# Attention and a top-1 mixture of experts on one core: routing steps kept in line, three batches counted, scatters between products, gate sums on ScalarE and VectorE

## The chip, the core and the metric

The kernel runs on one core of a Trainium2 chip. The metric is the device time of one execution in microseconds (us), as the median of several runs. A core has TensorE (PE, matrix products), VectorE (DVE), ScalarE (ACT), GpSimd (POOL), SyncE (SP, which here issues most of the DMAs) and DMA queues. Each engine follows its own list of instructions, and semaphores make one wait for another.

## What is computed

Cut to what matters:

```python
# attention: q, k, v are (8, 8, 576, 64): batches, heads, positions, width
scores = (1 / sqrt(64)) * q @ k.transpose(0, 1, 3, 2)
scores = where(block_i >= block_j, scores, -1e9)      # blocks of 64 positions
scores = scores - scores.max(-1, keepdims=True)
attn = exp(scores); attn = attn / (attn.sum(-1, keepdims=True) + 1e-9)
x = (attn @ v) .transpose(0, 2, 1, 3).reshape(4608, 512)
# top-1 mixture of 8 experts
logits = x @ w_gate + modality_bias[modality_id]      # w_gate is 512 x 8
e_idx = argmax(logits, axis=1)
probs = exp(logits - max); probs /= probs.sum(-1) + 1e-9
gate_w = probs[arange(N), e_idx]
for e in range(8):                                    # w1 is 512 x 1024, w2 1024 x 512
    mask = e_idx == e
    h = maximum(x[mask] @ w1[e], 0)
    out[mask] = gate_w[mask, None] * (h @ w2[e])
```

The tokens are routed by what attention gives, so the gate's sums, the choice of the expert and the place of each token in its expert's list are worked out while attention still runs.

## The kernel before

**Attention in slots.** The 64 heads make 32 pairs; four pairs are a batch of 576 tokens. One pair enters per slot, and slot n works on pair n and on what is left of pair n - 1. The table `ORDER` sets the order in which a slot's pieces are written, and a manual schedule keeps each engine to it: S0 to S3 scores (TensorE, L202), M0 to M4 maxima (VectorE, L209 and L211), E0 to E4 exponentials (ScalarE, L222), V the value products of the previous pair (TensorE, L248), O its turn_out (ScalarE, two copies, L256 and L257), Q the scaling of the next pair (POOL, L184, four instructions), T0 to T5 transposes (TensorE, L229) into six PSUM banks, C0 to C5 copies of these to SBUF (L234: groups 0, 1 and 5 on VectorE, 2, 3 and 4 on ScalarE), D an inverse (VectorE, L274 and L275), B the back products of the previous pair, which turn its output and multiply it with its part of the gate's weights (TensorE, L268), Z0 and Z1 the rows and gate terms of the previous pair (VectorE, L287 and L288). Bank 0 and bank 1, which C0 and C1 read, are what the next slot's S0 and S1 write.

**Routing.** When a batch's last pair has its rows (Z1), `routing(b)` gives a list of steps. Those that are left of the earlier list are first run at once, in a bulk. The places q1 to q6 in `ORDER` take one step each in passing (three where the step belongs to `choose`); qv and qp are for steps that need a certain place. In slot 4b + 5 the list begins: `logits` sums the gate terms of four pairs (VectorE, L314), `total` adds the two heads of a pair (TensorE, L317), `biased` adds the bias (VectorE, L321 to L324), `top` and `shifted` and so on lead to an exponential (ScalarE, L336), counts, and places in the lists. Its last step hands five scatters of token numbers (`indirect_dma_start` on POOL, L395, each with an index from VectorE, L394) to a queue `placing`, from which S0 and T0 of the following slots take one each.

**Choosing early.** After `EARLY` = 4 batches `choose` (22 instructions of 8 columns, on VectorE; in the trace they have the line L99 of a helper) picks the two fullest experts. `EARLY_STEPS` then stage their weights by DMA (L641, L644), and `prep` splits them on POOL (L584, L585), beginning in slot 21. Token rows for the first expert slots are fetched by gathers (L667) from slot 30 on.

**Experts.** `LAST` is the slot after the last pair: it mixes the end of attention with the first upward products (L706), and `run_all` goes on with 256 tokens at a time: up, relu (L712, L713), turned rows of the next tokens (L688 to L692), down (L752), scaled rows scattered to the output (L755). The routing of the last batch is still to be done there; `flush` then runs what is left in `placing` in one row. The lists of the experts are read (L662) after that.

```python
            if name == "Z1" and p % PPB == PPB - 1:
                for f in steps:
                    f()
                steps = routing(p // PPB)
                if p // PPB == EARLY - 1:
                    choose(Later(dve, steps))
```

## Time and profile before

| | |
|---|---|
| Time, median of 3 runs | 749.65 us (749.33 to 749.71) |
| The profiled execution | 747.08 us, span 745.4 us |
| TensorE busy | 724.3 us, 97% |
| VectorE, ScalarE, POOL busy | 345.0 us (46%), 332.2 us (45%), 242.6 us (33%) |
| Attention, slots 0 to 31 | to about 294 us of the span |

Slots are told by the start of their first score product: slot 17 begins at 154.17, slot 21 at 189.26, slot 22 at 200.02, slot 30 at 273.19, slot 31 at 283.29. A row of a timeline may gather several instructions of one kind that follow each other; its second number is then the time that all of them took. The idle time in brackets ended with what stands behind the arrow.

### The profile page before, as it was taken

Reading aid. Unit: us, or ns where it says so; the run is one execution under the profiler, and the core shown is the slowest. Engines: PE = TensorE matmul, PEld = TensorE weight load, DVE = VectorE, ACT = ScalarE, POOL = GpSimd, SP = SyncE. Lnnn points to the kernel's source line nnn. Section 1 sums busy time; section 2 is a strip of 40 time slices with the busy share of each in tenths; the row PEclk is TensorE's granted clock in tenths of the full one; section 3 lists DMA queues with packets and bytes.
Section 4 is the critical chain, followed back from the end, with each engine's and each line's share of the span. In section 5 each row is a group of like instructions: output and inputs, shape, how many; then the busy total and the mean of one; then the engine's idle time right before and its main releaser. Section 6 shows DMA issues by size and latency. Waiting matters only on the chain. (4 is left out here: it accounts for less than half of the span.)

```text
span 745.4 us, 19432 instructions
## 1 busy us (share of the span) xinstructions
PE 724.3 (97%) x7800; PEld 633.5 (85%) x7800; DVE 345.0 (46%) x1036; ACT 332.2 (45%) x974; POOL 242.6 (33%) x326
## 2 busy tenths in 40 slices
PE   8999999999989999989999999999999999999995
PEld 5888888888778888978999889998899988999794
DVE  4888888988989987421221112211222122221220
ACT  5888877888767876212222222221222222221220
POOL 2223343433399964155223132232111221112101
PEclk9999999999999999998999999999999999999998
DMA  5476456464667672313221222213121221201000
GB/s 183 127 213 215 125 165 168 138 177 137 156 194 238 197 209 78 90 34 73 78 79 36 79 72 86 72 43 100 50 79 48 81 86 45 84 30 47 29 15 20
DMA packets 41916, 77.80 MB, mean 104 GB/s; under 512 B 12170, under 2 KB 24266, under 8 KB 41824
## 3 DMA queue, kind: packets, MB, share of 16 engines
q1 hardware_dynamic: 34336, 57.02, 26.3%
q0 software_dynamic: 7488, 19.52, 8.4%
q8 instruction: 62, 1.02, 0.6%
q14 instruction: 30, 0.25, 0.1%
HBM read 54.86 MB, written 22.25 MB: 103 GB/s over the span
## 5 line engine op out<-in xcount | busy, mean ns | idle before, releaser
L713 DVE SCALAR_TENSOR_TENSOR extra<-bank,extra 128x512 fp32r<-128x512 f32 x72 | 49.8, 692 | 313.8 <-ACT extra L712 313.8
L222 ACT ACTIVATE pm<-bank,nm 128x512 f32<-128x512 f32 (+3 forms) x320 | 155.6, 500 | 64.9 <-DVE nm L209 60.0
L209 DVE TENSOR_REDUCE nm<-bank 128x1 f32<-128x512 f32 (+3 forms) x320 | 121.0, 447 | 6.5 <-PE bank L202 6.0
L706 PE MATMUL bank<-extra 128*128 128x256 f32 x960 | 119.4, 285 | 2.7 <-issue 2.7
L706 PEld LDWEIGHTS bank<-extra 128*128 128x128 f32 x960 | 117.7, 192 | 4.4 <-issue 3.6
L712 ACT ACTIVATE extra<-bank 128x512 fp32r<-128x512 f32 x72 | 43.1, 598 | 158.6 <-PE bank L706 149.1
L229 PE MATMUL bank<-cf,pm 128*128 128x128 f32 (+1 forms) x736 | 90.7, 279 | 3.3 <-ACT pm L222 3.3
L706 PE MATMUL bank<-extra,w0hb 128*128 128x256 f32 x512 | 91.1, 280 | 0.0
L202 PE MATMUL bank<-raw,q 64*64 64x512 f32 (+7 forms) x1280 | 87.8, 407 | 2.5 <-POOL q L184 2.5
L229 PEld LDWEIGHTS bank<-cf,pm 128*128 128x128 f32 (+1 forms) x736 | 79.5, 140 | 11.3 <-ACT pm L222 7.0
L184 POOL TENSOR_SCALAR q<-raw 128x144 f32<-128x144 f32 x124 | 67.7, 573 | 59.4 <-PE bank L229 47.9
L202 PEld LDWEIGHTS bank<-raw,q 64*64 64x64 f32 x1280 | 54.9, 134 | 30.2 <-issue 21.1
L706 PEld LDWEIGHTS bank<-extra,w0hb 128*128 128x128 f32 x512 | 79.0, 188 | 0.7
L248 PE MATMUL b<-pt,v 64*64 64x64 f32 (+3 forms) x896 | 77.0, 267 | 0.9 <-issue 0.6
L248 PE MATMUL o<-pt,v 64*64 64x64 f32 (+3 forms) x896 | 72.5, 262 | 1.0 <-issue 1.0
L706 PE MATMUL bank<-extra,w0lb 128*128 128x256 f32 x256 | 71.8, 280 | 0.0
L755 POOL DMA_INDIRECT out<-scratch,ids_b x17 | 16.9, 994 | 161.8 <-ACT scratch L754 161.8
L234 DVE COPY pt<-bank 128x512 f32<-128x512 f32 (+1 forms) x96 | 59.2, 642 | 21.2 <-PE bank L229 15.6
L222 ACT ACTIVATION_READ_ACCUMULATOR pm<-bank,nm 128x1 f32 x320 | 65.2, 204 | 0.0
L395 POOL DMA_INDIRECT idlist<-idt,pi x40 | 40.3, 1008 | 73.8 <-DVE pi L394 67.6
L248 PEld LDWEIGHTS b<-pt,v 128*64 128x64 f32 (+1 forms) x896 | 54.7, 136 | 3.9 <-issue 1.0
L752 PE MATMUL o<-extra 128*128 128x512 f32 x240 | 57.2, 394 | 0.0
(149 smaller groups left out, 992.0 us busy)
## 6 DMA issues: line engine op xcount, KB each, us to landing
raw<-qk SPq DMA_DIRECT2D x31, 576.0 KB
v<-vr SPq DMA_DIRECT2D x32, 384.0 KB
staging<-w SPq DMA_DIRECT2D x24, 256.0 KB
staging<-w SPq DMA_DIRECT2D x12, 512.0 KB
xrows<-xr SPq DMA_DIRECT2D x16, 256.0 KB
xrows<-xr SPq DMA_DIRECT2D x32, 128.0 KB
idlist<-btmp SPq DMA_DIRECT2D x8, 304.0 KB
xrows<-xr SPq DMA_DIRECT2D x16, 64.0 KB
```

What stands on the lines that cost most here:

```text
L184: pool.tensor_scalar(d.q[:, i : i + 144], d.raw[:, i : i + 144], SCALE, None, ALU.mult)
L202: pe.matmul(place(s, a, b)[64 * t : 64 * t + 64], d.q[hs, D * s : D * s + D], d.k[hs, a:b], start=True, stop=True)
L209: dve.tensor_reduce(d.nm[:, i : i + 1], place(s, a, b), AX.X, ALU.max, negate=True)
L222: act.activation(d.pm[:, o : o + b - a], place(s, a, b), AF.Exp, bias=d.nm[:, s : s + 1], scale=1.0, accum_out=total)
L229: pe.transpose(banks[g][0:m, 128 * i : 128 * i + 128], d.pm[:, o : o + m], idf)
L234: dve.tensor_copy(dst, src) if g in ON_DVE else act.copy(dst, src)
L248: pe.matmul(o.rearrange("p (n c) -> p n c", c=64), d.v[rows, h, block, :], x, start=start, stop=stop)
L395: last = pool.indirect_dma_start(idlist[:], bass.IndirectOffsetOnAxis(ap=g.pi[c], axis=0), g.idt[:, c, :], None, bounds_check=NROW - 1, oo ...
L706: nc.tensor.matmul(hp[:, a, :], w[:, kc, ms], x[:, kc, :], start=i == 0, stop=i == len(mm) - 1)
L712: self.nc.scalar.activation(hh, hp, AF.Relu)
L713: self.nc.vector.scalar_tensor_tensor(hl, hp, 0.0, hh, ALU.max, ALU.subtract)
L752: nc.tensor.matmul(y, s.hs[m][x][:, ts], self.part(w, 1, m // 2)[:, m % 2, :], start=n == 0, stop=n == len(mm) - 1)
```

## The change

- `total` is no longer a product. ScalarE copies the two halves of the sums crosswise into `sw`, and a new step `both` adds them on VectorE. `biased` may then stand at any q.
- Steps that are left of a list stay in line ahead of the next batch's (`steps + routing(...)`). While more than 20 are left, a q takes two; from slot 29 (`HURRIED`) on, three.
- `EARLY` is 3, and the first two staging transfers are issued at the start of slot 20.
- Scatters are taken at V and T3, and the fetches of token rows have other places. The first fetch has a buffer of its own (`xg0`).
- In `LAST` and `run_all` the last batches' scatters have places of their own, up to the first upward product of `run_all`; the lists are read after that product (`lists`).

```diff
-EARLY, NLEAD = 4, 3
+EARLY, NLEAD = 3, 3
+HURRIED = 29
...
-    (21, "S0"): ("stage", "stage"), (21, "T0"): ("prep",),
+    (20, "S0"): ("chosen", "stage", "stage"), (21, "T0"): ("prep",),
     **{(slot, "T0"): ("stage", "prep") for slot in range(22, 29)},
-    (28, "S0"): ("ids",), (29, "S0"): ("stage",),
-    (30, "S0"): ("fetch",), (30, "T0"): ("fetch",),
-    (31, "S0"): ("fetch",), (31, "T0"): ("fetch",),
+    (28, "S0"): ("ids",), (29, "T3"): ("fetch",), (30, "S0"): ("stage",), (30, "T0"): ("fetch",), (31, "T0"): ("fetch",),
 }
 LAST = (
-    ("+turn0", 0), ("V", 1), ("O", 1), ("D", 1), ("+up0", 0), ("+relu", 0), ("B", 1), ("Z0", 1), ("Z1", 1), ("+place", 0), ("+up1", 0), ("+relu", 0), ("+up2", 0), ("+steps3", 0), ("+up3", 0), ("+place", 0),
-    ("+relu", 0), ("+relu", 0), ("+turn1", 0), ("+steps2", 0),
+    ("+turn0", 0), ("V", 1), ("O", 1), ("D", 1), ("+up0", 0), ("+relu", 0), ("+fetch", 0), ("B", 1), ("Z0", 1), ("Z1", 1), ("+steps1", 0), ("+up1", 0), ("+relu", 0),
+    ("+place", 0), ("+steps14", 0), ("+up2", 0), ("+relu", 0), ("+place", 0), ("+steps5", 0), ("+up3", 0), ("+place", 0), ("+relu", 0), ("+turn1", 0),
 )
...
         def total():
-            pe.matmul(tot, ii, g.l0, start=True, stop=True)
+            g.sw = t([128, NSUB, NE], name="sw")
+            act.copy(g.sw[0:64], g.l0[64:128])
+            act.copy(g.sw[64:128], g.l0[0:64])
+
+        def both():
+            g.tot = t([128, NSUB, NE], name="tot")
+            dve.tensor_tensor(g.tot, g.l0, g.sw, ALU.add)
...
-        total.kind = counts.kind = "qp"
-        biased.kind = running.kind = "qv"
+        counts.kind = "qp"
+        running.kind = "qv"
...
-            if placing and slot < NPAIR and name in ("S0", "T0"):
+            if placing and slot < NPAIR and name in ("V", "T3"):
...
-                for _ in range(1 if kind else 3 if quick else 1 + (slot == PPB * EARLY + 1)):
+                for _ in range(1 if kind else 3 if quick else 3 if slot >= HURRIED else 1 + (len(steps) > 20)):
...
-                for f in steps:
-                    f()
-                steps = routing(p // PPB)
+                steps = steps + routing(p // PPB)
...
-        self.down(s, 0)
-        for f in steps[0:9]:
-            f()
-        self.down(s, 1)
-        for f in steps[9:]:
-            f()
-        self.flush()
...
+        for i in range(2):
+            self.early("place")
+            self.down(s, i)
...
+                    if n == 1:
+                        self.early("place")
+            if n == 1:
+                self.lists()
```

How this moves the instructions is seen in their order on the engines. First VectorE in slot 17, from the end of M4 (`nm` are the maxima, `l` the gate sums, `pi` a scatter's index, `pt` what C0, C1 and C5 write from banks 92, 93 and 97, `den` and `inv` the inverse, `xr` the rows). Before:

```order
L211 TENSOR_TENSOR nm<-nm 128x1
L314 TENSOR_REDUCE l_2701<-gl 128x72
L394 TENSOR_TENSOR pi_2533<-pp,cf 128x1
L234 COPY pt_111<-bank_92 128x512
L234 COPY pt_111<-bank_93 128x512
L274 SCALAR_TENSOR_TENSOR den<-sums,long_66 128x9
L275 RECIPROCAL inv<-den 128x9
L234 COPY pt_111<-bank_97 128x384
L287 TENSOR_TENSOR xr_81<-o_98,inv 128x5x64
L288 TENSOR_TENSOR gl<-o_98,inv 128x40
```

After:

```order
L210 TENSOR_TENSOR nm<-nm 128x1
L398 TENSOR_TENSOR pi_2431<-pp,cf 128x1
L312 TENSOR_REDUCE l_2743<-gl 128x72
L321 TENSOR_TENSOR tot<-l_2743,sw 128x72
L325 TENSOR_TENSOR lg<-tot,bias 64x32
L326 TENSOR_TENSOR lg<-tot,bias 64x16
L327 TENSOR_TENSOR lg<-tot,bias 64x16
L328 TENSOR_TENSOR lg<-tot,bias 128x8
L233 COPY pt_111<-bank_92 128x512
L233 COPY pt_111<-bank_93 128x512
L273 SCALAR_TENSOR_TENSOR den<-sums,long_66 128x9
```

`both` (`tot`) and the four instructions of `biased` stand ahead of the two copies from banks 92 and 93 now; before, `biased` came in the next slot, behind the first maximum. On ScalarE, in the same slot, the two copies into `sw` stand here after the change (`pm` are the exponentials, `ot` is turn_out's tile):

```order
L221 ACTIVATE pm_109,long_67<-bank_97,nm 128x64
L255 COPY ot<-o_98 128x256
L256 COPY ot<-b_99 128x320
L316 COPY sw<-l_2743 64x72
L317 COPY sw<-l_2743 64x72
L233 COPY pt_111<-bank_94 128x512
```

They have come between turn_out and the copies C2 to C4. POOL from slot 29 on, with the scaling of pair 30 (`q_102`, in slot 29) and of pair 31 (`q_103`, in slot 30): `idlist` is what scatters write, `xr` and `extra` what gathers write. Before:

```order
L184 TENSOR_SCALAR q_102<-raw_100 128x144 x4
L395 DMA idlist<-idt,pi_4487 38912x16
L395 DMA idlist<-idt,pi_4488 38912x16
L667 DMA xr_81<-xrows,row 128x528
L184 TENSOR_SCALAR q_103<-raw_101 128x144 x4
L395 DMA idlist<-idt,pi_4489 38912x16
L667 DMA xr_81<-xrows,row 128x528 x2
L373 COPY wt<-sm 128x80
L667 DMA xr_81<-xrows,row 128x528
L667 DMA xr_81<-xrows,ids_lead 128x528 x2
```

After, from the scatter ahead of these on:

```order
L399 DMA idlist<-idt,pi_4509 38912x16
L672 DMA xr_81<-xrows,ids_lead 128x528 x2
L399 DMA idlist<-idt,pi_4510 38912x16
L183 TENSOR_SCALAR q_102<-raw_100 128x144 x4
L377 COPY wt<-sm 128x80
L399 DMA idlist<-idt,pi_4511 38912x16
L672 DMA extra<-xrows,row 128x528
L399 DMA idlist<-idt,pi_4512 38912x16
L183 TENSOR_SCALAR q_103<-raw_101 128x144 x4
L672 DMA extra<-xrows,row 128x528
L399 DMA idlist<-idt,pi_4513 38912x16
L399 DMA idlist<-idt,pi_4863 38912x16
```

The gathers with `ids_lead` are those of the third fetch; they stood behind all of attention and now stand ahead of the scaling of pair 30 in slot 29. Last, POOL in the expert part, with the scatters to `out` of the first downward products. Before:

```order
L755 DMA out<-scratch,ids_lead 4608x512
L373 COPY wt<-sm 128x80
L755 DMA out<-scratch,ids_lead 4608x512
L395 DMA idlist<-idt,pi_5153 38912x16
L395 DMA idlist<-idt,pi_5154 38912x16
L395 DMA idlist<-idt,pi_5155 38912x16
L395 DMA idlist<-idt,pi_5379 38912x16
L395 DMA idlist<-idt,pi_5380 38912x16
L395 DMA idlist<-idt,pi_5381 38912x16
L395 DMA idlist<-idt,pi_5382 38912x16
L395 DMA idlist<-idt,pi_5383 38912x16
L661 TENSOR_LOAD di_r
```

After:

```order
L399 DMA idlist<-idt,pi_4866 38912x16
L399 DMA idlist<-idt,pi_4867 38912x16
L399 DMA idlist<-idt,pi_5298 38912x16
L760 DMA out<-scratch,ids_lead 4608x512
L399 DMA idlist<-idt,pi_5299 38912x16
L760 DMA out<-scratch,ids_lead 4608x512
L399 DMA idlist<-idt,pi_5300 38912x16
L655 TENSOR_TENSOR w0lb<-staging_79,w0hb 128x1024
L399 DMA idlist<-idt,pi_5301 38912x16
L399 DMA idlist<-idt,pi_5302 38912x16
```

The scatters to `idlist`, of which eight stood in a row behind the second one to `out`, are now among the scatters to `out` and a conversion of weights (`w0lb`).

## Rows read from the trace of the kernel before

**Rows 1.** The page, busy time by engine: busy us, share of the span, instructions.
```profile
PE 724.3 (97%) x7800; PEld 633.5 (85%) x7800; DVE 345.0 (46%) x1036; ACT 332.2 (45%) x974; POOL 242.6 (33%) x326
```

**Rows 2.** Table by stretches: length, busy time by engine, then TensorE's granted clock, DMA share, GB/s.
```profile
154.17:163.10 8.93, 8.93 (x172) 7.72 (x166) 7.73 (x24) 7.46 (x27) 4.21 (x6) 1.00 0.62 138
163.10:171.98 8.88, 8.88 (x169) 7.17 (x164) 7.84 (x30) 6.71 (x26) 4.84 (x8) 1.00 0.81 268
180.70:189.26 8.56, 8.56 (x170) 7.14 (x165) 8.08 (x34) 6.71 (x25) 1.28 (x2) 1.00 0.41 118
189.26:200.02 10.76, 9.28 (x172) 7.38 (x166) 9.64 (x43) 7.32 (x27) 4.21 (x6) 1.00 0.64 153
200.02:211.69 11.67, 9.16 (x171) 7.30 (x161) 9.71 (x35) 7.68 (x27) 7.56 (x13) 1.00 0.95 270
273.19:283.29 10.10, 9.46 (x168) 7.71 (x160) 8.49 (x33) 7.53 (x27) 4.22 (x6) 1.00 0.69 215
283.29:293.88 10.59, 9.65 (x166) 7.99 (x158) 8.06 (x28) 7.40 (x26) 4.41 (x5) 1.00 0.26 60
322.41:340.08 17.67, 14.99 (x100) 14.21 (x99) 6.00 (x33) 3.31 (x5) 12.72 (x13) 0.81 0.10 19
351.89:363.25 11.36, 11.36 (x97) 11.36 (x96) 2.08 (x3) 3.42 (x5) 4.43 (x3) 1.00 0.08 27
```

**Rows 3.** Timeline of VectorE, slot 17: start, busy, engine, line, operation, count, idle before.
```profile
159.63 0.45 DVE L314 TENSOR_REDUCE l<-gl 128x72 f32<-128x288 f32 x1
...
160.46 1.29 DVE L234 COPY pt<-bank 128x512 f32<-128x512 f32 x2 [0.33 <-PE bank L229]
...
162.53 0.56 DVE L234 COPY pt<-bank 128x384 f32<-128x384 f32 x1 [0.46 <-PE bank L229]
...
163.48 0.49 DVE L287 TENSOR_TENSOR xr<-o,inv 128x320 f32<-128x320 f32 x1 [0.39 <-DMA xrows<-xr]
...
164.49 0.68 DVE L209 TENSOR_REDUCE nm<-bank 128x1 f32<-128x512 f32 x1
...
165.09 0.17 DVE L321 TENSOR_TENSOR lg<-b,bias 64x32 f32<-64x32 f32 x1
```

**Rows 4.** Timeline of ScalarE, slots 17 and 18.
```profile
161.62 0.46 ACT L257 COPY ot<-b 128x320 f32<-128x320 f32 x1
...
165.21 0.69 ACT L222 ACTIVATE pm<-bank,nm 128x512 f32<-128x512 f32 x1 [1.68 <-DVE nm L209]
...
171.19 0.28 ACT L336 ACTIVATE ex<-df 128x40 f32<-128x40 f32 x1
```

**Rows 5.** Timeline of VectorE and POOL, slot 17: an index and its scatter.
```profile
159.99 0.15 DVE L394 TENSOR_TENSOR pi<-pp,cf 128x1 int32<-128x1 f32 x1
...
160.42 1.03 POOL L395 DMA_INDIRECT idlist<-idt,pi  x1 [1.31 <-DVE pi L394]
```

**Rows 6.** Timeline of POOL, slot 22.
```profile
203.56 0.39 POOL L584 CAST extra<-staging 128x256 fp32r<-128x256 f32 x1 [5.15 <-DMA staging<-w]
...
209.45 2.19 POOL L184 TENSOR_SCALAR q<-raw 128x144 f32<-128x144 f32 x4
```

**Rows 7.** Timeline of VectorE (first and last of 13) and ScalarE, slot 21.
```profile
190.84 0.22 DVE L99 SCALAR_TENSOR_TENSOR kx<-cnb,mx_b,cf 128x8 f32<-128x8 f32 x1
...
192.58 0.17 DVE L99 SCALAR_TENSOR_TENSOR start<-oh_b,begin 128x8 f32<-128x8 f32 x1
...
193.46 0.69 ACT L222 ACTIVATE pm<-bank,nm 128x512 f32<-128x512 f32 x1 [3.44 <-DVE nm L209]
```

**Rows 8.** Timeline of POOL, slot 29.
```profile
269.35 2.20 POOL L184 TENSOR_SCALAR q<-raw 128x144 f32<-128x144 f32 x4
```

**Rows 9.** Timeline of POOL (first and last of 8) and ScalarE, first upward product.
```profile
324.79 0.97 POOL L395 DMA_INDIRECT idlist<-idt,pi  x1 [0.30 <-DVE kx_c L413]
...
333.72 0.97 POOL L395 DMA_INDIRECT idlist<-idt,pi  x1 [0.30 <-issue]
...
336.46 0.60 ACT L712 ACTIVATE extra<-bank 128x512 fp32r<-128x512 f32 x1 [9.51 <-remote]
```

More of the change, by code (lines that the diff above doesn't have):

```diff
@@ L400, in place_sum @@
             placing.extend((scatter, c) for c in range(5))
-        return [logits, total, biased, top, shifted, hits, expo, hit_index, first, onehot, weight, weight_guard, weight_out, stores, counts, running, place_run, place_pick, place_sum]
+        return [logits, total, both, biased, top, shifted, hits, expo, hit_index, first, onehot, weight, weight_guard, weight_out, stores, counts, running, place_run, place_pick, place_sum]
     sel = {}
@@ L501, in run_slot @@
                 if ex is None:
-                    ex = Experts(ctx, tc, cst, scratch, btmp, con["edges"], xrows, idlist, idf, w1, w2, out, sel, run, base8, pick, dot, banks, (o0, banks[5]), placing, staging, extra, xrb)
+                    ex = Experts(ctx, tc, cst, scratch, btmp, con["edges"], xrows, idlist, idf, w1, w2, out, sel, run, base8, pick, dot, banks, (o0, banks[5]), placing, staging, extra, xrb, lambda kind: any(getattr(f, "kind", "") == kind for f in steps))
                 ex.early(what)
@@ L547, with __init__ @@
 class Experts:
-    def __init__(self, ctx, tc, cst, scratch, btmp, edges, xrows, idlist, idf, w1, w2, out, sel, run, base8, pick, dot, banks, ys, placing, staging, extra, xrb):
+    def __init__(self, ctx, tc, cst, scratch, btmp, edges, xrows, idlist, idf, w1, w2, out, sel, run, base8, pick, dot, banks, ys, placing, staging, extra, xrb, steps_left):
         self.__dict__.update(locals())
@@ L578, in early @@
             self.stage()
+        elif what == "chosen":
+            assert not self.steps_left("c")
         elif what == "prep":
@@ L670, in fetch @@
         s = Pair()
-        s.xg, s.ids, s.t, s.name, s.parts, s.hp, s.hs = self.xg[self.turn % 2], ids, t, name, parts, [], []
+        s.xg, s.ids, s.t, s.name, s.parts, s.hp, s.hs = self.xg[self.turn % 2] if self.turn else self.xg0, ids, t, name, parts, [], []
         self.turn += 1
@@ L774, in trips, with lists @@
         return counti
[L776 to L792 removed]
+    def lists(self):
+        cst, sel, dve = self.cst, self.sel, self.nc.vector
         self.flush()
[L794 removed]
         self.rem, left = (cst.tile([128, NE], F32, name=n) for n in ("rem", "left"))
@@ L803, in run_all @@
         self.more = self.trips(left)
-        plan += [(idsa, 2 * t, "a") for t in range(NSLOT - NLEAD)]
-        plan += [(idsb, 2 * t, "b") for t in range(NSLOT - 1)]
-        plan += [(idsb, 2 * NSLOT - 2, "b", N, 1), (idsc, 0, "a")]
-        for n in range(1, len(plan)):
+        self.plan += [(idsa, 2 * t, "a") for t in range(NSLOT - NLEAD)]
+        self.plan += [(idsb, 2 * t, "b") for t in range(NSLOT - 1)]
+        self.plan += [(idsb, 2 * NSLOT - 2, "b", N, 1), (idsc, 0, "a")]
+    def run_all(self, steps):
+        tc, ctx, plan = self.tc, self.ctx, self.plan
+        self.wk = wk = ctx.enter_context(tc.tile_pool(name="wk", bufs=1, side="right", reuse_waits="tile"))
+        self.w["b", 0] = [wk.tile([128, 4, DF], F32R, name=f"w0{x}b") for x in "hl"]
+        wk.tile([128, SHIFT], F32R, name="pad0")
+        w2 = [wk.tile([128, 2, DM], F32R, name=f"w1b{i}") for i in range(8)]
+        wk.tile([128, SHIFT], F32R, name="pad1")
+        self.w["b", 1] = [w2[0:4], w2[4:8]]
+        assert not steps
+        s, nxt = self.parts
+        later = self.fetch(*plan[2])
+        for i in range(2):
+            self.early("place")
+            self.down(s, i)
+        s, nxt = nxt, later
+        count = 2 * NSLOT + 1
+        for n in range(1, count):
             if s.parts == 1:
```

23 lines of the change are left out of this document (5 added, 18 removed).

## The prediction

> **What bounds the kernel now.** I read the page first: TensorE is busy for 97% of the span [rows 1], so a gain can only come from places where it waits or runs slowly, and a loss from every new wait put in its way. The table by stretches comes next. The attention part is 32 slots of nearly one length. A plain slot takes 8.56 us; the one that begins a batch's routing takes 8.93 and the one after it 8.88 [rows 2]. TensorE is busy throughout those. Three kinds of stretch stand out: slots 21 and 22 (10.76 and 11.67), slots 30 and 31 (10.10 and 10.59), and the first upward product of the expert part, 17.67 against 11.36 for the same product later, with 14.99 busy and a granted clock of 0.81 in it.
>
> Then I read slot 17 engine by engine, since the same slot recurs for every batch. VectorE copies banks 0 and 1 (C0, C1) at 160.46, copies group 5 at 162.53, waits 0.39, writes the rows of the previous pair from 163.48, and only then begins the next slot's maxima at 164.49 [rows 3]. ScalarE does the exponentials without a break, ends with turn_out at 161.62 + 0.46 = 162.08, and after its three copies stands idle for 1.68 until VectorE's first maximum [rows 4]. So a slot is a ring: turn_out (ScalarE), back products (TensorE), rows and first maximum (VectorE), exponentials (ScalarE), turn_out. Its length is the slot's length, and TensorE's own work is hardly shorter. What delays VectorE between the fourth maximum and the rows delays the ring.
>
> **Part 1: the gate sums.** Before, `total` is one product pair on TensorE and `biased` stands on VectorE between the first two maxima of the next slot: 165.09 to about 165.73, four instructions [rows 3]. After, ScalarE makes two copies of 64 x 72 into `sw`, which stand behind both halves of turn_out, and VectorE's `both` and `biased` stand ahead of C0 and C1. VectorE's instructions run in the order in which they are written, so C0 waits for turn_out. Worked out from slot 17 (start 154.17): turn_out ends at +7.91. The price of the copies is not in the trace; the nearest rows are a 128 x 40 activation of 0.28 and turn_out's 0.46 [rows 4]. Two of them, overlapping as ScalarE's rows do, take 0.2 to 0.6; I take 0.36, near the small one: +8.27. `both` costs about a 40-element row, and `biased` the 0.64 above: C0 starts at +8.95 instead of +6.29. C0 and C1 take 1.29 (+10.24), inverse, top and the scatter's index about 0.4, C5 0.56, the rows 163.48 to 164.49 1.01: the next first maximum comes at about +12.26 instead of +10.32, or 1.94 later. `biased` no longer lies between the next slot's maxima, which gives back the 0.33 by which 8.88 exceeds 8.56 [rows 2]. Net +1.6 in each of batches 0, 1, 3, 4 and 5: **+8.0**. The bounds: nothing, if the wait is covered (first rival), and +2.1 for each with the dearer copies. TensorE cannot use the wait, since its next product writes the bank that C0 reads.
>
> Here a rule of the Trainium skill speaks for the change. "Perfetto Trace Analysis", section "Identifying the Most-Contended Engine", says that kernels mostly improve by relieving the most contended engine; TensorE is that one here, so taking a product from it for two engines that are half idle would be a gain of the product's length. The rows above say that the half-idle engines are links of the ring, so that their order counts and not their share; by the rule this part's term would be below nothing, by the rows +8.0.
>
> In slots 13 and 29, more steps are taken for each place, so the copies stand ahead of the last exponentials and all of `biased`, `top` and `shifted` ahead of C0. Batch 2 (slots 13 and 14) gets **+0.8**: two copies on ScalarE's stretch, 0.36, and about as much on VectorE; bounds 0 and 1.6. Slot 29 is in part 4.
>
> **Part 2: scatters at V and T3.** In slot 17 an index ends at 159.99 + 0.15 and POOL's scatter begins at 160.42 and takes 1.03 [rows 5]. A scatter at V has its index right behind the last maximum, about 0.4 earlier because the reduction `logits` (0.45) is no longer ahead of it: it ends near +6.9. The scaling of the next pair stands behind it on POOL and takes 2.19, and the next slot began 0.05 after its end in slot 22 [rows 6]: +9.1 to +9.2. In the slots of part 1 that is hidden, since C0 frees its bank at +9.6. In slots 10, 22 and 26 it is not: 8.55 to 8.88 would become 9.0 to 9.3, about 0.4 each, **+1.2** (bounds 0 and 2.1).
>
> **Part 3: three batches counted.** The 22 small instructions of `choose` go from slots 20 and 21 to 15 and 16. Before, the last 13 run in a bulk ahead of slot 21's maxima, from 190.84 to 192.67, and ScalarE idles 3.44 for the first maximum [rows 7]; slot 21 is 10.76 against 8.56 to 8.88 [rows 2], so **-2.1**. After, 7 stand ahead of C0 in slot 15 and 9 in slot 16; at 1.83 / 13 = 0.14 each that is 2.2 in the ring, **+2.2** (bounds +0.8, if the waits ahead of C0, 0.33 each [rows 3] and the rest, absorb part of them, and +3). The staging transfers are issued in slot 20 instead of 21. Before, POOL waited 5.15 for the first one, preparation then held the scaling until 209.45, which took 2.19, and slot 22 ended 0.05 later, at 211.69 [rows 6]. A slot earlier that wait is gone: 11.67 - 8.88 = **-2.8** (bounds -2.8 and 0, if the transfer is held by something else in its queue).
>
> **Part 4: slots 29 to 31 and LAST.** Three steps for each place put nearly all of batch 6's routing of a slot ahead of C0, which adds about as much as in slots 15 and 16, 2.2. The scatters and gathers get other places, which may give back part of the 1.5 and 2.0 by which slots 30 and 31 (10.10 and 10.59) exceed a plain one [rows 2]. But the scheduler also draws two gathers of the third fetch ahead of the scaling in slot 29, and they wait for the stores of batch 6's rows. Before, that scaling ran from 269.35 to 271.55 [rows 8], and the next slot began at 273.19: the gathers, at about 1.3 each as the scatters of [rows 9] follow each other, use up the 1.64 between, and what their wait adds is on the path unless VectorE is later still. Bounds -1.3 (2.2 less all 3.5) and +4 (2.2, the gathers' excess of 1.0 and half a scaling's 2.19 of waiting, estimates); I take **+1.3** for the slots, in the middle, and **+0.2** for the added wait for counts in LAST (about one small instruction, 0.17 as in [rows 3]).
>
> **Part 5: the run of scatters.** Before, eight scatters stand in one row on POOL from 324.79 to 333.72, and in this stretch TensorE stutters, its clock falls and ScalarE waits 9.51 for a product [rows 9]: the product takes 17.67 instead of 11.36, so 6.3 is to be had [rows 2]. After, they are spread over the downward products, one or two at a time. Single scatters cost nothing that shows: slot 17 has one at 160.42 [rows 5], and TensorE is busy through all of it [rows 2]. Why a run costs, the trace doesn't tell. Bounds: -6.3 (all back) and -1 (the later pairs stutter too). I take **-4.5**, nearer the full amount, since what is left of the run is nearer to single scatters.
>
> **The sum.** 8.0 + 0.8 + 1.2 - 2.1 + 2.2 - 2.8 + 1.3 + 0.2 - 4.5 = +4.3. The rows come from the execution of 747.08 us (span 745.4); that becomes 751.4. The median of the runs shown is 749.65, 2.57 above it, so I add to that: **754.0 us**.
>
> **Rivals.**
> Faster: the wait for `sw` is covered. By the Trainium skill's rule in "Perfetto Trace Analysis", "Identifying the Most-Contended Engine", it would come out so. Place: C0 in the slots of batches 0, 1, 3, 4 and 5. If ScalarE reaches the copies so that C0 is not late, or other slots' slack takes it up, the term is 0 less 0.33 a batch: -1.7 instead of +8.0, and the sum is -5.4, **744.2**; with all 6.3 of part 5 it is 742.4. The point from which it decides: below 0.74 for each batch (4.3 lies 3.7 below 8.0) the kernel is faster. ScalarE's half-empty share speaks for it, the unbroken exponentials up to turn_out against it. Chance 0.18.
> No change: the wait is there, but the run of scatters gives back all its 6.3, slots 29 to 31 cost nothing and `choose` costs 1 of its 2.2: 4.3 - 1.8 - 1.3 - 1.2 = 0, **749.6**. Chance 0.15.
> Slower still: POOL's scatters hurt TensorE wherever two stand together, so part 5 gives 1, and the gathers in slot 29 hold the scaling, for +3.0 in part 4: 4.3 + 3.5 + 1.7 = 9.5, **759**. The slots 30 and 31 of before speak for it. Chance 0.15.
>
> **How the numbers follow.** My forecast has 0.5: 754.0, its own range 751.5 to 757. A measurement of this kernel tells 0.2% (1.5 us) from no change. The faster rival and small ends of the forecast give 0.20 for faster, the second rival 0.13 for the same, the rest 0.67 for slower. The range leaves out the far half of the first rival and the last end of the third: 744 to 759.
>
> **What would show it.** In the changed kernel slots 9, 17, 21 and 25 should be near 10 us or push the following slot, with VectorE idle more than 2 us ahead of `both`, released by ScalarE, and C0 at about +9. Slot 22 should have no wait for staging, slot 21 no bulk, slots 15 and 16 a late C0. POOL's scaling should end slots 10, 22 and 26. The first upward product should come near 11.4 to 13 at full clock. I am wrong if `both` waits less than 0.7, if slots 29 to 31 fall by several us, or if the stutter of the first upward product comes back elsewhere.

## The result and the profile after

The changed kernel takes **754.99 us** (median of 4 runs, 753.5 to 755.64); the kernel before, in the runs beside it, 749.49. The ratio is 1.0078, with a 95% interval of 1.0053 to 1.0103. Forecast were 754.0 and slower. The median is 5.5 above that of the kernel before; 4.3 was forecast. The profiled execution has a span of 751.9 us where that of before has 745.4, so the rows below have to account for +6.5.

The table by stretches of the changed kernel: slots 17, 18, 22, 29 and 30, the first upward product of `run_all`, and an upward product of the second expert (columns as in [rows 2]).

```profile
161.21:170.81 9.60, 8.81 (x155) 7.30 (x156) 6.74 (x24) 7.88 (x28) 4.26 (x6) 1.00 0.71 167
170.81:180.12 9.31, 9.31 (x153) 7.22 (x157) 8.77 (x31) 6.22 (x25) 4.32 (x8) 1.00 0.63 215
208.74:219.50 10.76, 10.76 (x153) 8.09 (x155) 10.01 (x33) 6.92 (x26) 6.88 (x12) 0.84 0.62 196
275.02:288.13 13.11, 10.41 (x173) 8.07 (x164) 11.13 (x43) 8.53 (x30) 8.67 (x14) 1.00 0.89 245
288.13:298.33 10.20, 10.20 (x153) 7.83 (x155) 7.03 (x25) 7.04 (x25) 5.49 (x8) 0.84 0.48 130
338.37:349.73 11.36, 11.36 (x97) 11.36 (x96) 2.27 (x6) 3.42 (x5) 5.37 (x4) 1.00 0.09 28
546.64:557.85 11.21, 11.21 (x97) 11.20 (x96) 2.07 (x3) 2.48 (x4) 3.06 (x3) 1.00 0.24 73
```

Against [rows 2], slot 17 has grown from 8.93 to 9.60 and slot 18 from 8.88 to 9.31, slot 22 has shrunk from 11.67 to 10.76, and the first upward product from 17.67 to 11.36. Slot 29 stands out with 13.11; before, it took 8.77 (from 264.42 to 273.19). Slots 9 and 25, which like slot 17 begin a batch's routing, have grown more than slot 17: to 10.44 and 10.66 from 8.93 and 8.96. The last row is 11.21; the same product before took 11.39:

```profile
560.62:572.01 11.39, 11.39 (x97) 11.39 (x96) 2.07 (x3) 2.48 (x4) 3.05 (x3) 1.00 0.24 71
```

That row isn't one that the forecast had looked at. VectorE in slot 17 of the changed kernel, from the end of the maxima to the next slot's:

```profile
166.25 0.44 DVE L312 TENSOR_REDUCE l<-gl 128x72 f32<-128x288 f32 x1
...
169.20 0.23 DVE L321 TENSOR_TENSOR tot<-l,sw 128x72 f32<-128x72 f32 x1 [2.51 <-ACT sw L317]
...
170.03 1.28 DVE L233 COPY pt<-bank 128x512 f32<-128x512 f32 x2
...
171.67 0.55 DVE L233 COPY pt<-bank 128x384 f32<-128x384 f32 x1
...
172.24 0.48 DVE L286 TENSOR_TENSOR xr<-o,inv 128x320 f32<-128x320 f32 x1
...
173.18 2.21 DVE L208 TENSOR_REDUCE nm<-bank 128x1 f32<-128x512 f32 x5
```

`both` (`tot`) waited 2.51 us for ScalarE's second copy. The first of C0 and C1 starts at +8.82 after the slot's start (161.21), and the next first maximum at +11.97; before, these were +6.29 and +10.32 [rows 3]. ScalarE in the same place:

```profile
168.18 0.46 ACT L256 COPY ot<-b 128x320 f32<-128x320 f32 x1
...
168.66 0.25 ACT L316 COPY sw<-l 64x72 f32<-64x72 f32 x1
...
168.92 0.25 ACT L317 COPY sw<-l 64x72 f32<-64x72 f32 x1
...
173.90 0.69 ACT L221 ACTIVATE pm<-bank,nm 128x512 f32<-128x512 f32 x1 [3.14 <-DVE nm L208]
```

The two copies take 0.25 each and stand behind turn_out, as the order showed; from turn_out's end (168.64) to `both` it is 0.56. Then ScalarE stands idle for 3.14 until the next maximum, where it was 1.68 [rows 4].

The 6.5 us are found by marks of the program, at their start (slots by their first score product, us from the span's start):

```
                                  before   after
slot 2                             23.49   23.28
slot 29                           264.42  275.02
LAST (first turned rows)          293.88  308.90
first upward product of run_all   322.41  338.37
the downward products behind it   340.88  350.52
second expert, first product      514.01  523.66
end                               745.39  751.86
```

From slot 2 to slot 29 the changed kernel takes 10.8 longer, from slot 29 to LAST 4.4, in LAST, with the first downward products behind it, 0.9. The first upward product gives back 6.3, and the second expert 3.2. The rest is equal to 0.2.

### The profile page after: what moved, and what is told of

Read it like the earlier page. It is cut to its first block, busy times and chain, and to the rows that moved or that the text cites. A ratio compares the mean times of both kernels' runs of the same rounds, so it can differ in the third digit from the quotient of the medians.

```text
span 751.9 us, 19402 instructions
## 1 busy us (share of the span) xinstructions
PE 726.4 (97%) x7784; PEld 629.4 (84%) x7784; DVE 350.7 (47%) x1044; ACT 337.1 (45%) x990; POOL 243.3 (32%) x326
## 3 DMA queue, kind: packets, MB, share of 16 engines
q8 instruction: 62, 1.02, 0.6%
## 5 line engine op out<-in xcount | busy, mean ns | idle before, releaser
L711 PEld LDWEIGHTS bank<-extra 128*128 128x128 f32 x960 | 115.1, 188 | 1.0 <-issue 0.2
L711 PE MATMUL bank<-extra 128*128 128x256 f32 x960 | 115.8, 281 | 0.0
L201 PE MATMUL bank<-raw,q 64*64 64x512 f32 (+7 forms) x1280 | 93.5, 419 | 8.6 <-POOL extra L589 4.0
L228 PE MATMUL bank<-cf,pm 128*128 128x128 f32 (+1 forms) x736 | 93.4, 280 | 3.9 <-ACT pm L221 3.0
L201 PEld LDWEIGHTS bank<-raw,q 64*64 64x64 f32 x1280 | 56.6, 137 | 41.2 <-issue 23.0
L247 PE MATMUL o<-pt,v 64*64 64x64 f32 (+3 forms) x896 | 70.6, 262 | 0.3 <-issue 0.2
```

The costliest lines, as they stand in the source:

```text
L201: pe.matmul(place(s, a, b)[64 * t : 64 * t + 64], d.q[hs, D * s : D * s + D], d.k[hs, a:b], start=True, stop=True)
L228: pe.transpose(banks[g][0:m, 128 * i : 128 * i + 128], d.pm[:, o : o + m], idf)
L247: pe.matmul(o.rearrange("p (n c) -> p n c", c=64), d.v[rows, h, block, :], x, start=start, stop=stop)
L711: nc.tensor.matmul(hp[:, a, :], w[:, kc, ms], x[:, kc, :], start=i == 0, stop=i == len(mm) - 1)
```

## The experiments

Each one is an edit of the changed kernel, if nothing else is said; the diffs are cut. All ratios are to the kernel before, run beside it on the same chip. The chips differ: the kernel before has medians of 747.2 to 749.5 on all but one, and 739.24 on that one, where only the run with the last batch's steps was made. So what a run gains on the changed kernel is told by the two ratios (that of the changed kernel is 1.0078), in us of 749.5, or by the marks of the profiled executions. The stretches between the marks:

```
                              slots 2   slot 29   LAST to     first    second
                              to 28     to LAST   upward    upward    expert
before                         240.9      29.5      28.5      18.5     231.4
after                          251.7      33.9      29.5      12.2     228.2
gate sums on TensorE           241.3      33.1      31.9      12.2     231.5
`both` late                    245.4      32.7      30.4      12.2     228.2
scatters at S0 and T0          247.2      32.4      28.9      12.2     228.2
gate sums and scatters undone  238.9      32.3      30.9      12.2     228.3
`both` late, S0 and T0         241.2      33.1      32.6      12.2     228.2
before with the unused tile    242.7      29.8      28.5      18.4     228.4
third fetch at the end         251.7      31.2      28.8      12.2     228.4
all of it                      239.0      28.6      28.8      12.2     228.3
```

"First upward" is from the first upward product of `run_all` to the downward products behind it.

**Gate sums on TensorE again.**

```diff
         def total():
-            g.sw = t([128, NSUB, NE], name="sw")
-            act.copy(g.sw[0:64], g.l0[64:128])
-            act.copy(g.sw[64:128], g.l0[0:64])
-
-        def both():
-            g.tot = t([128, NSUB, NE], name="tot")
-            dve.tensor_tensor(g.tot, g.l0, g.sw, ALU.add)
+            g.tot = b0[:, TABLE : TABLE + NSUB * NE].rearrange("p (s e) -> p s e", s=NSUB)
+            pe.matmul(g.tot, ii, g.l0, start=True, stop=True)
...
-        counts.kind = "qp"
-        running.kind = "qv"
+        total.kind = counts.kind = "qp"
+        biased.kind = running.kind = "qv"
```

Expected: 

> The changed kernel with the gate sums as before: one product pair on TensorE, biased between the next slot's first two maxima; nothing else undone. My theory (VectorE's wait for ScalarE's copies delays the ring of a slot): slots 9 and 10, 17 and 18, 25 and 26 lose most of their excess (together 2.5, 1.1 and 2.9 us in the changed kernel), some 8 us in all, so about 747; no 2.5 us wait of VectorE ahead of C0 is left. Rival (TensorE is the bound, and a product off it is a gain): about 2 us slower than the changed kernel, 757. A side question: with the constant back, tiles stand at the addresses of the kernel before. If the products of the second expert were faster in the changed kernel (upward 11.20 instead of 11.39) because of addresses, they are 11.39 again here and the time is 3 us higher than else, about 750.

The constant `ii` comes back with it, and LAST takes 13 steps for 14, since the list is one shorter.

Measured: 747.18 (745.77 to 748.24, 10 runs), ratio 0.9984 (0.9974 to 0.9995), 7.0 less than the changed kernel. From slot 2 to slot 29 it takes 10.5 less, but in LAST 2.4 more and in the second expert 3.3 more. An upward product of the second expert takes what it took before the change:

```profile
607.33:618.72 11.39, 11.39 (x98) 11.39 (x97) 2.08 (x3) 2.48 (x4) 3.05 (x3) 1.00 0.24 71
```

So, with the scatters at V and T3, the gate sums cost even more than the 8 us of the theory: TensorE got its product back and the kernel is 1% faster. The Trainium skill says in "Perfetto Trace Analysis", "Identifying the Most-Contended Engine", that the most contended engine is to be optimized first; read as the prediction reads it, that a product off TensorE is a gain, this run should be slower, and it is not. The side question has its answer too: with the old addresses, the second expert is slow again (231.5 to the end, as before).

**`both` behind the next slot's first maximum.**

```diff
             dve.tensor_tensor(g.tot, g.l0, g.sw, ALU.add)
-
-        def biased():
...
-        running.kind = "qv"
+        both.kind = running.kind = "qv"
```

Expected: 

> The changed kernel with ScalarE's copies kept, but both and biased in one step that stands behind the next slot's first maximum. My theory (the wait is what costs, not the copies): slots 9, 17, 21 and 25 come back to about 9, and the sum falls by some 6 us, to about 749. If ScalarE's copies themselves cost (0.5 us ahead of C2 to C4 in the ring), it falls by 2 or less, to 753 or more.

Measured: 747.8 (745.62 to 750.36, 10 runs), ratio 1.0003 (0.9985 to 1.0021), 5.6 less than the changed kernel. VectorE in slot 22, where `both` now comes without a wait:

```profile
204.50 0.69 DVE L208 TENSOR_REDUCE nm<-bank 128x1 f32<-128x512 f32 x1 [0.26 <-PE bank L201]
205.10 0.60 DVE L321 TENSOR_TENSOR tot<-l,sw 128x72 f32<-128x72 f32 x1
```

ScalarE's copies are still there; what has gone is the place in VectorE's order at which their result is awaited, and with it the four instructions of `biased` ahead of C0. The wait is most of the cost. Slots 9, 21 and 25 come back to 9.5, 9.5 and 8.9; slot 17 does not (9.9, where the changed kernel has 9.6), but it takes 9.9 with TensorE's product too.

**Scatters at S0 and T0 again.**

```diff
-            if placing and slot < NPAIR and name in ("V", "T3"):
+            if placing and slot < NPAIR and name in ("S0", "T0"):
```

Expected: 

> The changed kernel with scatters taken at S0 and T0 again instead of V and T3. My theory (a scatter at V stands ahead of the scaling of the next pair, which then ends the slot): slots 10, 14, 16, 22 and 26 get shorter, by 0.4 to 1 us each, 2 to 4 us in all, about 752. Rival (the slots end with VectorE anyway): no change, 755.

Measured: 745.95 (745.25 to 746.84, 6 runs), ratio 0.9967 (0.9954 to 0.9979): 8.3 less than the changed kernel, where I had expected 3. In the profiled executions it is 4.5 less from slot 2 to slot 29, a further 1.4 less from there to LAST and 0.6 in LAST, 6.7 in all; the profiled execution is the fastest of four of the changed kernel and the slowest of six here, so the profiles show less than the ratios. In the changed kernel POOL shows what happens, here in slot 10, which ends at 105.35:

```profile
102.11 0.97 POOL L399 DMA_INDIRECT idlist<-idt,pi  x1 [4.38 <-PE bank L228]
103.11 2.19 POOL L183 TENSOR_SCALAR q<-raw 128x144 f32<-128x144 f32 x4
```

A scatter, the four instructions of the scaling behind it (until 105.30), and 0.05 later the next slot. Slots 14, 16, 22, 26, 29 and 30 end in the same way, at most 0.06 behind the scaling.

That isn't all. Slots 9, 13 and 21 gain 0.5, 0.5 and 1.2 as well, and they do not end with the scaling. At the beginning of slot 9, which starts at 85.04 in the changed kernel and at 84.92 here, POOL and VectorE show, first in the changed kernel and then here (VectorE alone):

```profile
84.50 1.09 POOL L399 DMA_INDIRECT idlist<-idt,pi  x1 [8.14 <-DVE pi L398]
86.06 0.49 DVE L286 TENSOR_TENSOR xr<-o,inv 128x320 f32<-128x320 f32 x1 [0.85 <-PE o L267]
```

```profile
85.30 0.49 DVE L286 TENSOR_TENSOR xr<-o,inv 128x320 f32<-128x320 f32 x1 [0.21 <-PE o L267]
```

While a scatter taken at T3 is on POOL, VectorE waits 0.85 for the back products and begins the previous pair's rows at +1.02 instead of +0.38, and the whole ring of that slot comes 0.6 later. Slots 13 and 21 show the same. Why the scatter does this, the traces don't tell.

**The last scatters in one row.** Three kernels. The first has six of them in a row behind the second downward product, the second one eight (with the places of scatters in `LAST` gone too), the third eight and the lists read ahead of the upward product as before. The edit of the first in `run_all`:

```diff
         for i in range(2):
-            self.early("place")
             self.down(s, i)
+        self.flush()
```

Expected of six: 

> The changed kernel with the last six scatters in one row behind the downward products, as before, while the lists are still read after the first upward product. Theory that the row of scatters makes TensorE stutter: the first upward product of the expert loop takes 15 to 17.7 us instead of 11.4, with a lower granted clock, and the time is about 760. Rival (the reading of the lists ahead of that product was what cost): 11.4 as in the changed kernel, 755.

Expected of eight: 

> The changed kernel with the last eight scatters in one row behind the second scatter to the output, as many as before, and the lists still read after the product. With six in a row the first upward product lost 0.9 us. If the loss is that of the number in the row, it is some 5 to 6.5 us here, with a lower granted clock, and the time about 760; if the reading of the lists takes part in it, it stays below 2 and the time below 757.

Expected of eight with the lists: 

> The changed kernel with the last eight scatters in one row, as in the run with eight, and the lists read ahead of the first upward product, as before the change. With the row alone that product took 2.6 us more than undisturbed. If the reading of the lists ahead of it (and VectorE's steps for it) makes the rest of the 6.3, it takes some 17.7 here and the time is 759 to 760; if not, about 14 and 756, and the rest of the 6.3 stays open.

Measured: 753.57, 755.93 and 756.39; ratios 1.0075 (1.0059 to 1.0092), 1.0104 (1.0088 to 1.0119) and 1.0117 (1.01 to 1.0134). From the first upward product to the downward one it is 13.06, 14.76 and 14.90, against 12.15 in the changed kernel, and in every version with spread scatters on the same chips, and 18.47 before. With eight, POOL's first and last scatter of the row, and what TensorE did at the product's end:

```profile
341.54 0.98 POOL L399 DMA_INDIRECT idlist<-idt,pi  x1 [0.31 <-issue]
...
350.50 0.97 POOL L399 DMA_INDIRECT idlist<-idt,pi  x1 [0.30 <-issue]
```

```profile
350.16 0.72 PE L711 MATMUL bank<-extra 128*128 128x256 f32 x4 [0.43 <-issue]
...
351.58 1.11 PE L711 MATMUL bank<-extra 128*128 128x256 f32 x5 [0.69 <-issue]
```

TensorE waits 0.43, 0.69 and so on for nothing that the profile shows, from 8.2 us after the row's first scatter on. So a row alone makes TensorE stutter, the more the longer it is, and the lists add 0.14 at most; but this explains 2.6 to 2.8 of the 6.3 that were lost before. The rest isn't one of chips: on the chip of the second kernel, the kernel before with the unused tile (below) takes 18.41 for this stretch.

**The last batch's steps near the row as well.**

```diff
-    ("+steps14", 0), ("+up2", 0), ("+relu", 0), ("+steps5", 0), ("+up3", 0), ("+relu", 0), ("+turn1", 0),
+    ("+steps5", 0), ("+up2", 0), ("+relu", 0), ("+up3", 0), ("+relu", 0), ("+turn1", 0),
...
             self.down(s, i)
+            for f in steps[9 * i : 9 + 5 * i]:
+                f()
```

Expected: 

> The version with eight scatters in one row and the lists read ahead of the product (756.4), and also the last batch's routing steps, from the exponential on, between and behind the two first downward products instead of in LAST, as in the kernel before. That makes the weights' stores, the loads of the token numbers and the counts fall close to the row. Theory that these are the rest of the loss: the stretch from the first upward product to its downward product goes from 14.9 to 17 or more, with a lower granted clock, and the time to 758 or more. Rival (they have no part in it): it stays at 14 to 15, and the rest of the 6.3 stays open.

Measured: 749.36 (749.0 to 749.81, 4 runs), ratio 1.0136 (1.0119 to 1.0153). This run was on another chip, on which the kernel before takes 739.24 (737.94 to 740.28, 7 runs) and not 746 to 750 as on all others. The row of eight is there, and TensorE runs through the product without a gap:

```profile
336.66 0.98 POOL L399 DMA_INDIRECT idlist<-idt,pi  x1 [0.31 <-DVE kx_c L417]
...
345.60 0.97 POOL L399 DMA_INDIRECT idlist<-idt,pi  x1 [0.30 <-issue]
```

```profile
334.27 11.61 PE L711 MATMUL bank<-extra 128*128 128x256 f32 x96
```

It was 12.24 to the downward product, as in the changed kernel with its scatters spread: in this run the row costs nothing. The run differs from the one with the lists in two things, the steps and the chip. That the chip matters is seen in the attention part, which the edit leaves alone. Slot 9 starts at 84.98 here, with the scatter on POOL as in the changed kernel:

```profile
84.44 1.08 POOL L399 DMA_INDIRECT idlist<-idt,pi  x1 [8.03 <-DVE pi L398]
85.36 0.49 DVE L286 TENSOR_TENSOR xr<-o,inv 128x320 f32<-128x320 f32 x1 [0.21 <-PE o L267]
```

VectorE's rows begin at +0.38 and not at +1.02, in slots 13 and 21 too; the seven other versions with a scatter there, on other chips, all have +1.00 to +1.05. So the run doesn't answer what it was for: the missing 3.6 us (6.3 - 2.7) stay open. It suggests that part 5 is a gain on some chips only; no trace of the kernel before on this chip shows it.

**Gate sums and scatters undone together**, with a tile of 640 bytes (`sml.tile([128, 160], F32, name="moved", bufs=1)`) that is never used.

Expected: 

> The changed kernel with both of the parts undone that cost each 8 to 9 us alone: gate sums on TensorE, scatters at S0 and T0; and with a tile of 640 bytes that is never used, so that the second expert's weights lie as far from the other tiles as in the changed kernel. If the two costs are of different places, they add: attention to slot 31 falls from 298.3 to about 282 and the whole to 736 to 739. If they are one and the same wait seen twice (either one removes it), the time is that of one alone, 745 to 747.

Measured: 740.07 (739.47 to 742.06, 4 runs), ratio 0.9905 (0.9887 to 0.9922). They are two costs: 8.3 us from slot 2 to slot 29 for the gate sums when the scatters are at S0 and T0, 4.5 for the scatters. Of the 8.3, slots 5 and 6 have 1.2, slots 9 and 10 1.7, 17 and 18 0.6, 21 and 22 1.7, 25 and 26 1.6. Slot 30 takes 14.0 here; on POOL and VectorE there:

```profile
268.87 1.10 POOL L668 DMA_INDIRECT xr<-xrows,ids_lead  x1 [0.18 <-issue]
270.28 1.03 POOL L668 DMA_INDIRECT xr<-xrows,ids_lead  x1 [0.30 <-issue]
271.62 1.02 POOL L395 DMA_INDIRECT idlist<-idt,pi  x1 [0.30 <-issue]
272.94 1.02 POOL L668 DMA_INDIRECT extra<-xrows,row  x1 [0.31 <-issue]
```

```profile
274.80 0.49 DVE L287 TENSOR_TENSOR xr<-o,inv 128x320 f32<-128x320 f32 x1 [4.51 <-PE bank L202]
```

Four indirect transfers follow each other with 0.3 us between, and VectorE waits 4.51 for TensorE, whose score products take until 276.45, 6.15 us where they took 2.70 in slot 30 of the kernel before. The DMA engines are full all that time (a share of 1.01), but they were there before too (0.96). That fits the row as the cause; no run takes the row alone away.

**`both` late and scatters at S0 and T0**: the edits of the second and third experiment together.

Expected: 

> The changed kernel with both and biased behind the next slot's first maximum, and scatters at S0 and T0; ScalarE's copies stay. If ScalarE's copies cost next to nothing and the wait and the scatters all, about 739 to 741, 2 behind the version with TensorE's product; if the copies cost 0.5 in each of seven batches, 742 to 744.

Measured: 744.46 (743.17 to 745.47, 4 runs), ratio 0.9951 (0.9935 to 0.9967), 4.4 behind the version with TensorE's product. In the profiled executions 2.3 of it lie between slots 2 and 29, 0.8 between slot 29 and LAST, and 1.7 in LAST. So ScalarE's copies, or the steps that come later for them, aren't free either: of the 8.3 that the gate sums cost, some 6.0 (247.2 - 241.2) are the wait, with `biased`, and 2.3 the rest. The time is near the expectation's second case, a little above its 744.

**The kernel before with the unused tile**, and nothing else.

Expected: 

> The kernel before with a tile of 640 bytes that is never used, which moves all that lies behind it, the second expert's weights among it, and changes no instruction's order. Theory that the 3.2 us which the second expert's products take less in the changed kernel come from addresses: the stretch from its first slot to the end falls from 231.4 to 228.2 and the time to about 745 (ratio 0.996). Rival (they come from what the change does): 231.4 and no change.

Measured: 745.13 (744.07 to 746.53, 7 runs), ratio 0.9964 (0.9952 to 0.9977). An upward product of the second expert:

```profile
561.87:573.08 11.21, 11.21 (x99) 11.21 (x98) 2.07 (x3) 2.55 (x5) 3.06 (x3) 1.00 0.25 73
```

The same products at the same granted clock take 1.6% less, 228.4 from the second expert to the end instead of 231.4, because tiles stand elsewhere. What the changed kernel gained there comes from where its tiles lie, and not from the order of its work. (In this execution slots 2 to 28 take 1.7 longer than before, nearly all of it in slot 23; see the last section. A mark of one execution can be off by that much.)

**The third fetch at the end of LAST.**

```diff
-        s, nxt = self.parts
-        later = self.fetch(*plan[2])
+        s, nxt, later = self.parts
...
-    ("+relu", 0), ("+turn1", 0),
+    ("+relu", 0), ("+turn1", 0), ("+fetch", 0), ("+fetch", 0),
```

Expected: 

> The changed kernel with the third fetch's two gathers written at the end of LAST, so that none stands ahead of the scaling in slot 29. My theory of part 4 (VectorE's row of routing steps ahead of C0 makes slot 29 late, the gathers little more): slot 29 goes from 13.1 to about 12, and the time to about 754. Rival (the gathers, which wait for the stores of batch 6's rows, hold the scaling and so the slot): slot 29 falls to 11 or less and the time by 2 to 4, to 751 to 753.

Measured: 749.27 (748.71 to 750.39, 7 runs), ratio 1.0027 (1.0015 to 1.0038), 3.8 less than the changed kernel. Slots 29 and 30:

```profile
275.05:285.25 10.20, 9.36 (x171) 7.45 (x165) 9.14 (x32) 8.43 (x30) 6.56 (x11) 1.00 0.89 218
285.25:296.09 10.84, 9.88 (x171) 7.81 (x160) 9.68 (x37) 7.24 (x26) 5.57 (x8) 1.00 0.57 167
```

Slot 29 takes 10.2 instead of 13.1, though slot 30 then takes 10.8 instead of 10.2. The rival is right. POOL in slot 29 of the changed kernel, which ends at 288.13:

```profile
282.14 1.05 POOL L672 DMA_INDIRECT xr<-xrows,ids_lead  x1 [3.48 <-DMA xrows<-xr]
283.49 1.02 POOL L672 DMA_INDIRECT xr<-xrows,ids_lead  x1 [0.30 <-issue]
284.82 1.01 POOL L399 DMA_INDIRECT idlist<-idt,pi  x1 [0.31 <-DVE pt L233]
285.86 2.22 POOL L183 TENSOR_SCALAR q<-raw 128x144 f32<-128x144 f32 x4
```

The gathers wait 3.48 for the stores of batch 6's rows, and the scaling stands behind them and a scatter until 288.08.

**All of it**: gate sums on TensorE, scatters at S0 and T0, the unused tile, the third fetch in LAST, and one step for each place in slots 29 to 31 (`HURRIED = 99`), with `+steps5` in LAST for `+steps1`.

Expected: 

> The version with TensorE's gate sums, scatters at S0 and T0 and the unused tile (740.1), with the third fetch in LAST and one step for each place in slots 29 to 31, the last steps of batch 6 in LAST. In that version slot 30 took 14.0, with four indirect transfers in a row on POOL and VectorE waiting 4.5 us for a back product, and 13 us to C0. If these two cause it, slots 29 to 31 come to 8.8, 9 to 10.5 and 9.5 and the time to 735 to 737; if the wait in slot 30 is something else (the pair's raw data, say), it stays near 740.

Measured: **734.53** (734.22 to 734.63, 4 runs), ratio 0.9828 (0.9811 to 0.9844). Slots 29, 30 and 31:

```profile
261.62:271.11 9.49, 9.04 (x174) 7.61 (x165) 7.76 (x25) 7.81 (x27) 8.58 (x14) 1.00 0.64 144
271.11:281.43 10.32, 10.02 (x155) 7.57 (x156) 8.18 (x32) 6.86 (x26) 5.57 (x8) 1.00 0.68 207
281.43:290.23 8.80, 8.80 (x158) 7.51 (x159) 7.58 (x25) 7.16 (x26) 1.30 (x2) 1.00 0.20 44
```

This version keeps of the change the three batches, the steps in line and the spread scatters of the last batches, and beats both kernels. Some 2.8 of the 12.7 us that it is ahead of the kernel before are the unused tile's, by the run above.

## Why the prediction was right, and where it was not

The time was foreseen within 1 us and its sign for the main reason given, but several terms were off, and one was missing. The differences of marks, by the runs above (one execution each):

```
                                          forecast   measured
gate sums (batches 0 to 5)                   +8.8      +8.3
scatters at V and T3, slots 2 to 28          +1.2      +4.5
three batches counted, staging earlier       -2.7      -2.0
slots 29 to 31                               +1.3      +4.4
LAST                                         +0.2      +0.9
the row of scatters                          -4.5      -6.3
second expert's products                      0        -3.2
start, to slot 2                              0        -0.2
sum                                          +4.3      +6.5
```

The first three are read between slots 2 and 29. The scatters: the changed kernel less the one with scatters at S0 and T0 (251.7 - 247.2). The gate sums: that one less the one with both undone (247.2 - 238.9). The third: that one less the kernel before (238.9 - 240.9).

**Part 1, right in mechanism and sum, less so slot by slot.** The ring was the right picture. C0 was forecast at +8.95 and came at +8.82 in slot 17, the next maximum at +12.26 and came at +11.97. That these agree is partly luck: turn_out ended at +7.43 and not +7.91, while the copies took 0.25 each for the 0.18 taken, and `both` 0.23 where the forecast's +8.95 leaves it only 0.04. In slots 5, 9, 21 and 25 C0 came at +8.34, +9.66, +10.56 and +9.89. The term was 1.6 a batch, and it was worked out on slot 17, which paid least (0.6): with both costs undone it takes 9.82 and its first maximum comes late, at +2.45. The other four paid 1.2 to 1.7. Batch 2 paid 0.1 in slots 13 and 14 and 0.9 in the two behind them, for the 0.8 forecast.

**Part 2, the mechanism right, the size 3.3 too small.** The scaling behind a scatter does end slots. But I priced it on a slot whose last maximum ends at about +5.5, and on slots 10, 22 and 26 alone. In a slot that begins with a late ring the last maximum is later too, and the scatter and the scaling with it, so that the wait is passed on; slots 14 and 16 pay as well. With the gate sums on TensorE the scatters cost only 2.4 (241.3 - 238.9): 2 of the 4.5 are a product of both changes. And one mechanism was missing: a scatter at T3 delays the rows of slots 9, 13 and 21 by 0.6 each. The forecast had taken from slot 17 that single scatters cost nothing that shows.

**Part 3, right within 0.7.** With both costs undone, slots 21 and 22 take 18.3 where they took 22.4, 4.1 less for the 4.9 forecast, and slots 13 to 17 46.1 where they took 44.0, 2.1 more for the 2.2. In the changed kernel itself slot 21 has lost its bulk, though the wait for `sw` has come in its place (11.33 for 10.76), and POOL begins a preparation in slot 21 without waiting, from 206.80 on. But the second scatter and the scaling are no earlier than the maxima let them be:

```profile
206.80 0.41 POOL L589 CAST extra<-staging 128x256 fp32r<-128x256 f32 x1
...
217.24 2.21 POOL L183 TENSOR_SCALAR q<-raw 128x144 f32<-128x144 f32 x4
```

Slot 22 ends with that scaling again (219.45; the next slot begins at 219.50), so less of its 2.8 came back.

**Part 4, too small by 3.1, and outside its bounds (4.4 against +4).** I took the gathers ahead of the scaling as hidden behind VectorE for the most part. They are not: taking them away brings slot 29 from 13.1 to 10.2, and slots 29 to 31 from 33.9 to 31.2. I knew that they wait for the stores of batch 6's rows, and priced that wait at half a scaling; but the stores are only issued in that same slot (SyncE issues them from 275.92 to 282.3), and the first gather starts at 282.14.

**Part 5, right in kind, not in its cause's size.** All of the 6.3 came back. A row of six or eight makes TensorE stutter in the changed kernel too, but costs 0.9 and 2.6. What the other 3.6 came from, no run shows.

**Not foreseen: 3.2 from addresses.** The constant `ii` and the tiles `sw` and `tot` have moved the weights of the second expert against the tiles that are multiplied with them. This made up for half of what parts 2 and 4 cost more than forecast: without it, the changed kernel would have come out near 758, just outside the range (751.5 to 757).

So the mechanisms of the sum hold, but its closeness owes something to luck: misses of +3.3, +3.1 and twice +0.7 on one side, of -3.2, -1.8 and -0.7 (the gate sums and the start) on the other.

The sums have small slips that change no term: the pieces behind C0 add up to +12.21 and not +12.26, `choose` ends at 192.75 and not 192.67 [rows 7], the dearer copies give a bound of some +1.8 and not +2.1 a batch, and the upper bound of part 4 adds up to +4.3.

## What to carry to other kernels

An engine that is busy for 45% of the time may be the link that sets the pace: before work is moved to it, see what stands behind the new instruction in its order, and who waits for that. Two delays that each lie within the slack of a slot add up once one of them has used the slack (here 2.4 alone, 4.5 together), so a price from one undisturbed slot doesn't hold for all; price each slot that the change touches. And when a constant or a small tile comes or goes, compare stretches whose instructions didn't change: a difference there may be one of addresses, and a kernel before with an unused tile shows it in one run.

## What was not expected of the hardware

- **Addresses.** An unused tile of 640 bytes, which moves what lies behind it, changed a stretch of 96 products of 256 columns from 11.39 to 11.21 us in the kernel before, at the same granted clock; the changed kernel has 11.21 too, and 11.39 with its old constant back. Which distance is good, and why, no run shows.
- **Indirect transfers on POOL.** Six or eight of them in a row, 0.3 us apart, made TensorE pause for 0.3 to 0.75 us at a time, with no semaphore awaited, from 7.9 to 8.2 us after the first of the row. A single one, on POOL when a slot ended, made VectorE wait 0.6 longer for TensorE's back products. In the one run on the chip on which the kernel before takes 739.24, neither showed (the product took 11.61 at one go).
- **The clock after a wait.** In the changed kernel TensorE waits 2.12 us at the end of slot 21, and goes on at 208.74 (the row names POOL; but C0 and C1, VectorE's copies of the banks that slot 22's scores write, begin only at 207.97):

```profile
208.74 2.10 PE L201 MATMUL bank<-raw,q 64*64 64x512 f32 x8 [2.12 <-POOL extra L589]
```

From 209.60 to 212.60 its granted clock is 0.50, the 1.2 GHz level, and the work of slot 22 that lies there takes longer:

```profile
209.60:212.60 3.00, 3.00 (x22) 1.43 (x20) 3.00 (x11) 0.13 (x1) 2.76 (x4) 0.50 0.46 185
```

Slot 30 has the same share of it (0.84 in the first table), behind a wait of 1.32 us; no slot between 2 and 31 of the kernel before is below 1.00. But the length of the wait does not decide it. The kernel before waits 2.51 at the end of slot 22 and keeps 1.00; with the unused tile it waits 2.70 there, and the clock falls (the first row is slot 23 before, the second 3 us of it with the tile, in which it takes 10.28 instead of 8.59):

```profile
211.69:220.28 8.59, 8.59 (x155) 7.34 (x159) 6.87 (x20) 6.74 (x25) 8.06 (x15) 1.00 0.53 157
212.00:215.00 3.00, 3.00 (x27) 1.91 (x25) 1.91 (x4) 1.59 (x6) 2.82 (x6) 0.50 0.52 112
```

And the versions with eight scatters in a row, whose attention part is that of the changed kernel, wait the same 2.12 and 2.13 at the end of slot 21 and keep 1.00. What decides it, these runs don't show.
